# Expert weight sums on VectorE instead of GpSimd for the first two halves, and attention scores whose second term spans 128 partitions

## Chip, cores and metric

The program runs on one NeuronCore of a Trainium2 chip. The metric is the device time of one execution in microseconds. Before the change the median of three runs is 1225.96 us, from 1223.82 to 1226.51.

## What is computed

Three stages follow each other: attention with rotary position embedding, a gated feed-forward block, and a mixture of eight experts with a balanced gate.

```python
q_rot, k_rot = (rotate(q), rotate(k))          # batch 2, heads 8, 576 positions, 64 wide
scores = scale * np.matmul(q_rot, k_rot.transpose(0, 1, 3, 2))
attn = softmax(scores)                         # with +1e-9 in the denominator
x = heads_side_by_side(np.matmul(attn, v))     # 1152 x 512
a, b = x @ w1, x @ w2                          # 512 x 1024
x = ((a * b) @ w3) @ w_out                     # 1024 x 1024, 1024 x 512
P = np.exp(x @ w_gate - max)                   # 1152 x 8
for _ in range(8):
    P /= P.sum(1, keepdims=True) + 1e-09
    P /= P.sum(0, keepdims=True) + 1e-09
    P *= N / E
for e in range(8):
    out += P[:, e:e+1] * (np.maximum(x @ w1[e], 0) @ w2[e])   # 512 x 1024 x 512
```

## The kernel before

**Split numbers.** Every fp32 operand of a product is split into a high part in fp32r (a copy on ScalarE that rounds) and a low part (the difference). A product is three matmuls: high times high, high times low, low times high.

**Attention.** Two heads make a pair; there are 8 pairs, numbered 0 to 7. For each pair `load_qk` (L247) brings queries and keys with their half-swapped copies into a tile `raw` (two buffers, shared by queries and keys), `rope_mul` (L255) and `rope_add` (L259) rotate them on GpSimd, `rope_hi` (L269) makes the high part on ScalarE, and `rope_lo` the low part: for keys on GpSimd (L275), for queries on VectorE (L277). From pair 1 on, DMAs lay the parts out over 128 partitions: `spread_q` (L281) puts a head's high and low query parts one above the other in `sq`, and `spread_k` (L285) puts the head's high key part twice into `kk`, once beside each. So one matmul over 128 partitions gives high times high plus low times high. The remaining term, high query times low key, runs over the 64 partitions of the head alone: the low key part is written by `rope_lo` straight into slot 2 of `kk`, where the heads already lie on their own halves. `scores` (L312) therefore issues two matmuls of 128x128 by 288 columns and then two of 64x128 by 288 columns for each tile of 128 queries and each head; a "score step" below is these four. Pairs 1 to 7 have 5 tiles x 2 heads each, 70 score steps in all. Pair 0 takes its three terms over 64 partitions, six matmuls a step. Each step is followed by a row maximum on VectorE (L319), the exponential on ScalarE (L323), transposes on TensorE (L338), their copies out (L345) and the products with the values (L373, a 128x64 array tile).

**The order of attention** is not written by hand. The class `Plan` simulates the steps with fixed costs for each engine, ranks, and numbers of buffers (`kk` 2, `sq` 2, `raw` 2, `wide` 2 and so on) and emits the instructions in that order; each engine and the SP queue then run in that order. A step "takes" a buffer and "frees" one. The products of the two last dense weights (`w34_product`, L216 to L218) have the lowest rank and fill TensorE's gaps. Their operands come as 64-bit words and are converted by `wide_parts` on VectorE, ScalarE and GpSimd (L168 to L189).

**The experts** run as 16 steps s (expert e, half fh of the hidden width; s = 2e + fh). `prepare_first(s, u)` (L616) loads a quarter block of the first weight into `wide` (two buffers), forms four sums of 128x256 blocks into `sums` (one buffer, L625 to L628) for a seven-product scheme, and splits both into high and low parts (L125, L126). `hidden` (L681) multiplies, `project` (L729) applies the second weight and accumulates. For s = 0 `project` copies to `acc`; from s = 1 on it adds with the gate's weight (L746), so it needs the finished gate `pr`, and so does the scaling of `acc` by the first expert's weight (L835).

**The gate** is woven into step 0: `gate_start` (L778) takes one maximum over all partitions (L785) and `gate_round` (L789) runs eight times, each with one sum over all partitions, `partition_all_reduce` on GpSimd (L795), between small VectorE operations (L790 to L798). Outside attention the framework's scheduler decides the order of each engine's instructions.

Of the kernel before, what the change touches and what calls it, by code (L numbers as in the profile page):

```python
# [11 lines left out]
F32R = mybir.dt.float32r  # L12
# [94 lines left out]
def attention_two_moes(ctx: ExitStack, tc: tile.TileContext, rope, qk, v, mw12, mw3t, mwo, wg, ew1, ew2, out):  # L107
# [152 lines left out]

    def keys(n):
        if n not in K:
            K[n] = att_p.tile([P, 3, S], F32R, name="kk", bufs=2)
        return K[n]

    def rope_hi(n, w, c):
# [3 lines left out]

    def rope_lo(n, w, c, eng):
        t = raw[n, w]
        h, l = (t[:, 1, c], (t[:, 0, c].bitcast(F32R), keys(n)[:, 2])[w]) if n else (f32(QK0[w][:, 0, c]), QK0[w][:, 1, c])
        if w:
            eng.tensor_sub(l, t[:, 0, c], h)  # L275
        else:
            eng.scalar_tensor_tensor(out=l, in0=t[:, 0, c], scalar=QSCALE, in1=h, op0=ALU.mult, op1=ALU.subtract)  # L277
# [2 lines left out]

        sp.dma_start(f32(SQ[n % 2][half(x ^ j), j, :S]), raw[n, 0][half(j), 1 - x])  # L281

    def spread_k(n, j, x):

        sp.dma_start(f32(keys(n)[half(x), j]), raw[n, 1][half(j), 1])  # L285

    def half(j):
        return slice(j * D, (j + 1) * D)
# [5 lines left out]
    def scores(n, i, j):  # L294

        if j == 0:
            st["e", n, i] = att_p.tile([P, 2, S], F32, name="e", bufs=2)
            st["nm", n, i] = att_p.tile([P, 2], F32, name="nm", bufs=4)
            g, k, _ = group(i)
            if k == 0:  # L300
                st["sm", n, g] = att_p.tile([P, 3, 2], F32, name="sm", bufs=3)
        js = half(j)
        if n:
            q, k = SQ[n % 2][:, j], keys(n)
            terms = [(q, k[:, j]), (q[js], k[js, 2])]
        else:
            (qh, ql), (kh, kl) = ([t[js, x] for x in range(2)] for t in QK0)
            terms = [(qh, kh), (qh, kl), (ql, kh)]
        st["s", n, i, j] = ps = psS.tile([P, 2, 512], F32, name="s")
        for x, (q, k) in enumerate(terms):  # L310
            for h in range(2):
                pe.matmul(  # L312
                    ps[:, h, :HS], q[:, i * P : (i + 1) * P], k[:, h * HS : (h + 1) * HS],
                    start=(x == 0), stop=(x == len(terms) - 1),
                )
# [92 lines left out]
    for n in range(NP):  # L408
# [3 lines left out]
        for w in (1, 0):  # L412
            pieces = (slice(0, SF), slice(SF, S)) if n == w == 0 else (every,)
            for c in pieces:
                a, m = (n, w, c), c.stop - c.start
                r = t - 60.0 if n else -50.0 if c.start == 0 else -40.0
                r += 2 * (1 - w)
                rot = "pool" if n or c.start else "dve"
                tk = [("raw", (n, w))] if c.start == 0 else []
                step(load_qk, a, {"sp": 8 * P * m}, t - 60.0 - w if n else r - 40.0, takes=tk)  # L420
                step(rope_mul, a, {rot: 2 * m}, r, [(load_qk, *a), "tab"])
                step(rope_add, a, {rot: m}, r, [(rope_mul, *a)])
                tk = [(("sq", "kk")[w], n)] if n else []
                step(rope_hi, a, {"act": m}, r, [(rope_add, *a)], tk)
                fr = [("raw", (n, w))] if n == 0 and c is pieces[-1] else []
                step(rope_lo, a, {"pool" if n and w else "dve": m}, r, [(rope_hi, *a)], frees=fr + ([("raw", (n, 1))] if n and w else []))
            if n == 0:
                ready.append([(rope_lo, 0, w, c) for c in pieces])
                continue
            ready.append([(rope_lo, n, w, every)])  # L430
            for j, x in ((j, x) for j in range(2) for x in range(2)):
                if w:
                    step(spread_k, (n, j, x), {"sp": 4 * D * S}, t - 60.0, [(rope_hi, n, 1, every)], frees=[("raw", (n, 1))])
                else:
                    needs = [((rope_hi, rope_lo)[x], n, 0, every)]
                    step(spread_q, (n, j, x), {"sp": 4 * D * S}, t - 60.0, needs, frees=[("raw", (n, 0))])
                ready[-1].append(((spread_q, spread_k)[w], n, j, x))
        before = []
        for i in range(NQ):
            g, k, _ = group(i)  # L440
# [175 lines left out]
    def prepare_first(s, u):  # L616

        pl = wb_p if u else wa_p
        e, fh = divmod(s, 2)
        t = base.tile([P, 1024], F32, name="wide", bufs=2)  # L620
        sp.dma_start(t, ew1[e, 2 * fh + u])
        a11, a12, a22, a21 = (t[:, k * 256 : (k + 1) * 256] for k in range(4))
        sums = wa_p.tile([P, 1024], F32, name="sums")
        s1, s2, s3, s4 = (sums[:, k * 256 : (k + 1) * 256] for k in range(4))
        pool.tensor_add(s1, a21, a22)  # L625
        pool.tensor_sub(s3, a11, a21)
        pool.tensor_sub(s2, s1, a11)
        pool.tensor_sub(s4, a12, s2)  # L628
        W1[s, u] = []
        for src, n in ((t, 768), (sums, 1024)):  # L630
            h, l = (w_tile(pl, "w1") for _ in range(2))
            split_scalar_vector(h[:, :n], l[:, :n], src[:, :n])
            W1[s, u].append((h, l))
# [271 lines left out]
```

## Time and profile before

| | |
|---|---|
| median of three runs | 1225.96 us (1223.82 to 1226.51) |
| the profiled execution | 1230.79 us, of which the span of instructions is 1228.9 us |
| TensorE matmul busy | 1163.4 us, 95% of the span |
| TensorE weight loads busy | 1003.5 us, 82% |
| VectorE busy | 737.0 us, 60% |
| ScalarE busy | 427.1 us, 35% |
| GpSimd busy | 242.3 us, 20% |
| mean granted TensorE clock | 0.975 |
| score steps of pairs 1 to 7 | from 45.5 to 235.3 us |
| gate rounds | from 434.95 to 531.95 us |

Times are counted from the span's start. TensorE is busy for 95% of the whole, but that is a mean over stages: the stages with gaps, and what ends each gap, tell what a change in them is worth. A matmul's printed duration includes its way through the pipeline, so what a matmul costs TensorE is read from start to start. "PEld" is TensorE's weight load, which normally runs beside the matmul before. [...]

### The profile page before, as it was taken

What the parts mean: (1) busy time and instruction counts of PE and PEld (TensorE: products, weight loads), DVE (VectorE), ACT (ScalarE), POOL (GpSimd) and SP (SyncE); (2) the same over time, 40 slices, a digit from 0 to 9 for tenths busy, and PEclk for the clock granted to TensorE, in tenths of its full rate; (3) what the DMA queues carried; (4) which work ended last, traced back from release to release, by engine and by line L of the source; (5) the groups of instructions that cost most, each with busy time, mean ns of one, the idle gap of its engine ahead of it and who ended that gap; (6) DMA issues with size and microseconds to landing.
All of it is one profiled execution on the core that took longest, in us unless ns stands there. A gap on an engine that the chain in (4) does not pass through costs nothing.

```text
span 1228.9 us, 17324 instructions
## 1 busy us (share of the span) xinstructions
PE 1163.4 (95%) x6869; PEld 1003.5 (82%) x6869; DVE 737.0 (60%) x1324; ACT 427.1 (35%) x904; POOL 242.3 (20%) x239
## 2 busy tenths in 40 slices
PE   5889999898999999649999999999999999999998
PEld 4556666588999888638989989989889899889887
DVE  7887876587433383535665656656555655656643
ACT  3655666545332343202232232223222222322311
POOL 5646552042210001010010010010110100100100
PEclk9888999989999999869999999999999999999999
DMA  5545544054100010111111111111110111211102
GB/s 194 157 140 159 152 142 118 1 173 137 53 18 18 18 53 18 35 34 35 35 59 45 35 53 52 35 52 35 52 52 19 67 36 35 69 35 35 35 10 69
DMA packets 24993, 78.93 MB, mean 64 GB/s; under 512 B 3280, under 2 KB 3792, under 8 KB 24912
## 3 DMA queue, kind: packets, MB, share of 16 engines
q1 hardware_dynamic: 24768, 77.23, 19.9%
q8 instruction: 54, 0.88, 0.3%
q10 hardware_dynamic: 144, 0.59, 0.1%
q14 instruction: 27, 0.22, 0.1%
HBM read 67.19 MB, written 2.36 MB: 57 GB/s over the span
## 4 chain that ended last, share of the span: by engine, by line
PE 86%; DVE 6%; issue 5%; ACT 1%; POOL 1%; DMA 1%; POOLq 0%; DVEq 0%; ACTq 0%
PE z L738 11%; PE z L737 10%; PE z L739 10%; PE s L312 5%; PE T L696 4%; PE T L697 4%; PE T L698 4%; PE x L373 3%; PE t L338 3%; PE u L133 3%; PE u L131 3%; PE u L132 3%; PE Q L698 3%; PE Q L696 3%; PE Q L697 3%
## 5 line engine op out<-in xcount | busy, mean ns | idle before, releaser
L739 PE MATMUL z<-w,h 128*128 128x512 f32 x576 | 227.3, 395 | 0.0
L625 POOL TENSOR_TENSOR sums<-wide 128x256 f32<-128x256 f32 x32 | 26.8, 836 | 657.7 <-DVE w L126 335.5
L737 PE MATMUL z<-w,y 128*128 128x512 f32 x320 | 127.3, 398 | 18.6 <-DVE acc L746 18.6
L746 DVE SCALAR_TENSOR_TENSOR acc<-z,pr,acc 128x512 f32<-128x512 f32 x135 | 100.8, 748 | 56.9 <-PE z L739 56.8
L739 PEld LDWEIGHTS z<-w,h 128*128 128x128 f32 x576 | 108.6, 189 | 25.3
L738 PE MATMUL z<-w,y 128*128 128x512 f32 x320 | 127.0, 397 | 0.0
L737 PE MATMUL z<-w,h 128*128 128x512 f32 x256 | 101.5, 397 | 2.3 <-DVE acc L746 2.3
L738 PE MATMUL z<-w,h 128*128 128x512 f32 x256 | 102.0, 398 | 0.0
L125 ACT CAST w<-wide 128x768 fp32r<-128x768 f32 (+1 forms) x64 | 60.3, 943 | 94.3 <-PE z L738 62.4
L702 ACT ACTIVATE y<-tmp 128x320 fp32r<-128x320 f32 x96 | 45.0, 470 | 126.5 <-DVE tmp L718 77.4
L126 DVE TENSOR_TENSOR w<-wide,w 128x768 fp32r<-128x768 f32 (+1 forms) x64 | 69.7, 1089 | 30.0 <-ACT w L125 16.1
L702 ACT ACTIVATE h<-tmp 128x256 fp32r<-128x256 f32 x96 | 39.8, 416 | 122.1 <-DVE tmp L718 115.7
L737 PEld LDWEIGHTS z<-w,y 128*128 128x128 f32 x320 | 60.6, 189 | 25.5 <-DVE acc L746 19.0
L131 PE MATMUL u<-x,w 128*128 128x320 f32 (+1 forms) x256 | 76.8, 300 | 3.3 <-DVE gf L568 3.2
L133 PE MATMUL u<-x,w 128*128 128x320 f32 (+1 forms) x256 | 76.6, 299 | 0.0
L132 PE MATMUL u<-x,w 128*128 128x320 f32 (+1 forms) x256 | 76.1, 297 | 0.0
L338 PEld LDWEIGHTS t<-ident,e 128*128 128x128 f32 (+1 forms) x360 | 40.6, 149 | 37.0 <-issue 15.7
L319 DVE TENSOR_REDUCE nm<-s 128x1 f32<-128x576 f32 x80 | 59.6, 753 | 18.2 <-PE s L312 17.8
L312 PE MATMUL s<-kk,sq 128*128 128x288 f32 (+1 forms) x280 | 69.7, 351 | 0.2 <-ACT e L323 0.2
L338 PE MATMUL t<-ident,e 128*128 128x128 f32 (+1 forms) x360 | 59.2, 288 | 11.1 <-ACT e L323 8.2
L696 PE MATMUL T<-x,w 128*128 128x320 f32 x192 | 61.2, 319 | 5.3 <-ACT w L125 5.2
L738 PEld LDWEIGHTS z<-w,y 128*128 128x128 f32 x320 | 61.1, 191 | 6.2
(198 smaller groups left out, 3058.7 us busy)
## 6 DMA issues: line engine op xcount, KB each, us to landing
wide<-in_ew_dram SPq DMA_DIRECT2D x64, 512.0 KB, 3.5
raw<-in_qk_dram SPq DMA_DIRECT2D x15, 576.0 KB, 4.3
wide<-in_mw3t_dram SPq DMA_DIRECT2D x16, 512.0 KB, 4.6
wide<-in_mw_dram SPq DMA_DIRECT2D x16, 512.0 KB, 3.5
wide<-in_mwo_dram SPq DMA_DIRECT2D x8, 512.0 KB, 3.7
kk<-raw SPq DMA_DIRECT2D x28, 144.0 KB, 2.5
sq<-raw SPq DMA_DIRECT2D x28, 144.0 KB, 2.4
v<-in_v_dram SPq DMA_DIRECT2D x8, 320.0 KB, 4.1
```

Of the source, the lines that this page charges most:

```text
L131: pe.matmul(ps, wh, xh, start=(i == 0), stop=False)
L132: pe.matmul(ps, wh, xl, start=False, stop=False)
L133: pe.matmul(ps, wl, xh, start=False, stop=(i == n - 1))
L312: pe.matmul(ps[:, h, :HS], q[:, i * P : (i + 1) * P], k[:, h * HS : (h + 1) * HS], start=(x == 0), stop=(x == len(terms) - 1),)
L338: pe.transpose(ps[:, t, :rows], e[:rows, c : c + P], ident[:rows, :rows])
L696: pe.matmul(ps, h[:, ws], x[0], start=(first and k == 0), stop=False, **kw)
L697: pe.matmul(ps, h[:, ws], x[1], start=False, stop=False, **kw)
L698: pe.matmul(ps, l[:, ws], x[0], start=False, stop=(k == 1), **kw)
L737: pe.matmul(ps, hh[:, f, ts], wh, start=(f == 0), stop=False)
L738: pe.matmul(ps, hh[:, f, ts], wl, start=False, stop=False)
L739: pe.matmul(ps, hl[:, f, ts], wh, start=False, stop=(f == FT - 1))
L746: dve.scalar_tensor_tensor(out=acc[t], in0=ps, scalar=p, in1=acc[t], op0=ALU.mult, op1=ALU.add)
```

## The change

Two edits that touch no common code. First, for s = 0 and 1 the four block sums of `prepare_first` are issued on VectorE; from s = 2 on they stay on GpSimd. Second, the low key part is now written over the rotated key in `raw` and spread by four more DMAs per pair into two new slots of `kk`, twice like the high part. The second term of a score step becomes two matmuls over 128 partitions. It adds the product of both low parts, which before was left out. The `raw` buffer of the keys is now free when all eight spreads have landed; before it was free after four spreads and the low-part subtraction.

```diff
 def keys(n):
-            K[n] = att_p.tile([P, 3, S], F32R, name="kk", bufs=2)
+            K[n] = att_p.tile([P, 4, S], F32R, name="kk", bufs=2)
...
 def rope_lo(n, w, c, eng):
-        h, l = (t[:, 1, c], (t[:, 0, c].bitcast(F32R), keys(n)[:, 2])[w]) if n else (f32(QK0[w][:, 0, c]), QK0[w][:, 1, c])
+        h, l = (t[:, 1, c], t[:, 0, c].bitcast(F32R)) if n else (f32(QK0[w][:, 0, c]), QK0[w][:, 1, c])
...
-    def spread_k(n, j, x):
-
-        sp.dma_start(f32(keys(n)[half(x), j]), raw[n, 1][half(j), 1])
+    def spread_k(n, j, x, part):
+
+        sp.dma_start(f32(keys(n)[half(x), 2 * part + j]), raw[n, 1][half(j), 1 - part])
...
 def scores(n, i, j):
-            terms = [(q, k[:, j]), (q[js], k[js, 2])]
+            terms = [(q, k[:, j]), (q, k[:, 2 + j])]
...
                 if w:
-                    step(spread_k, (n, j, x), {"sp": 4 * D * S}, t - 60.0, [(rope_hi, n, 1, every)], frees=[("raw", (n, 1))])
+                    for part, made in enumerate((rope_hi, rope_lo)):
+                        step(spread_k, (n, j, x, part), {"sp": 4 * D * S}, t - 60.0, [(made, n, 1, every)], frees=[("raw", (n, 1))])
...
 def prepare_first(s, u):
-        pool.tensor_add(s1, a21, a22)
-        pool.tensor_sub(s3, a11, a21)
-        pool.tensor_sub(s2, s1, a11)
-        pool.tensor_sub(s4, a12, s2)
+        eng = dve if s < 2 else pool
+        eng.tensor_add(s1, a21, a22)
+        eng.tensor_sub(s3, a11, a21)
+        eng.tensor_sub(s2, s1, a11)
+        eng.tensor_sub(s4, a12, s2)
```

Lines after the edits lie two or three lower in the changed kernel: the sums are L628 to L631 there, the gate's reductions L788 and L798.

**GpSimd at the gate.** Before, the all-partition reductions (L785, L795, printed as ISA with an output) alternate with the block sums, and an ISA without an output stands at every change between the two kinds:

```order
L785 ISA
L785 ISA mg<-mx 128x1
L795 ISA cg<-cs 128x8 x2
L625 ISA
L625 TENSOR_TENSOR sums<-wide 128x256
L795 ISA
L795 ISA cg<-cs 128x8
L626 ISA
L626 TENSOR_TENSOR sums<-wide 128x256
L795 ISA
L795 ISA cg<-cs 128x8
L627 ISA
```

In the changed kernel the same place reads:

```order
L788 ISA
L788 ISA mg<-mx 128x1
L798 ISA cg<-cs 128x8 x8
L628 ISA
L628 TENSOR_TENSOR sums<-wide 128x256
```

All nine reductions now stand together; one ISA stands before them and one behind, and the first sum behind them belongs to s = 2.

**VectorE at the gate.** In the changed kernel the sums of s = 1, u = 0 stand between the splits of s = 0, u = 1 and the first sums of products (L712, in `hidden`):

```order
L126 TENSOR_TENSOR w_4243<-wide,w_4242 128x768
L126 TENSOR_TENSOR w_4247<-sums,w_4246 128x1024
L628 TENSOR_TENSOR sums<-wide 128x256
L629 TENSOR_TENSOR sums<-wide 128x256
L630 TENSOR_TENSOR sums<-sums,wide 128x256
L631 TENSOR_TENSOR sums<-wide,sums 128x256
L712 TENSOR_TENSOR tmp<-T,tmp 128x320
```

Before, L709 (the same line as L712) followed the two L126 directly; the four sums of s = 1, u = 1 are likewise strewn between later gate rounds.

**The SP queue between two pairs of attention.** Before (`kk` and `sq` are the spread keys and queries of one pair, the `raw` loads behind them bring the next):

```order
L285 DMA kk<-raw 64x576 x4
L247 DMA raw<-in_qk_dram 128x1152
L281 DMA sq_90<-raw 64x576 x3
L155 DMA wide<-in_mw3t_dram 128x1024
L281 DMA sq_90<-raw 64x576
L247 DMA raw<-in_qk_dram 128x1152
```

and in the changed kernel:

```order
L285 DMA kk<-raw 64x576 x8
L281 DMA sq_90<-raw 64x576 x4
L155 DMA wide<-in_mw3t_dram 128x1024
L247 DMA raw<-in_qk_dram 128x1152 x2
L251 DMA v_91<-in_v_dram 128x640
```

The next pair's keys were loaded behind four spreads; now both loads stand behind all twelve spreads.

## Rows read from the trace of the kernel before

**Rows 1.** Stretches: length, busy time (and count) of PE, PEld, DVE, ACT, POOL, granted clock, DMA

```profile
45.00:140.00 95.00, 87.99 (x463) 57.43 (x463) 76.72 (x108) 56.65 (x135) 54.20 (x35) 0.87 0.52 157
140.00:235.00 95.00, 94.85 (x570) 63.19 (x570) 65.25 (x116) 59.69 (x145) 34.38 (x25) 1.00 0.37 106
300.00:420.00 120.00, 120.00 (x901) 120.00 (x900) 48.09 (x100) 38.54 (x92) 11.42 (x12) 1.00 0.10 31
430.00:460.00 30.00, 29.86 (x198) 27.08 (x197) 25.11 (x74) 13.31 (x27) 3.03 (x5) 1.00 0.17 54
487.00:556.00 69.00, 42.52 (x212) 36.36 (x211) 31.08 (x77) 11.32 (x21) 8.33 (x13) 0.80 0.12 39
```

**Rows 2.** What TensorE waited for between 420 and 560 us: total, times, longest

```profile
PE z L737 <- DVE acc L746: 20.9, 2, 18.6
PE T L696 <- ACT w L125: 5.2, 1, 5.2
```

**Rows 3.** GpSimd's timeline at the gate: start, duration, operation, idle before it

```profile
478.84 0.73 POOL L627 TENSOR_TENSOR sums<-sums,wide 128x256 f32<-128x256 f32 x1 [7.32 <-issue]
485.80 1.29 POOL L795 PARTITION_ALL_REDUCE cg<-cs  x1 [6.23 <-issue]
495.12 0.71 POOL L628 TENSOR_TENSOR sums<-wide,sums 128x256 f32<-128x256 f32 x1 [8.04 <-issue]
...
531.52 0.43 POOL L795 PARTITION_ALL_REDUCE cg<-cs  x1 [6.23 <-issue]
```

**Rows 4.** First and last of the three busy stretches at half clock, columns as in rows 1

```profile
496.90:502.30 5.40, 5.34 (x19) 4.93 (x20) 1.77 (x3) 0.01 (x1) 0.00 (x0) 0.50 0.24 93
...
550.30:553.60 3.30, 3.30 (x12) 2.93 (x11) 0.58 (x2) 0.00 (x0) 0.00 (x0) 0.50 0.02 5
```

**Rows 5.** The chain that ended last, 45 to 238 us, by line

```profile
by line: PE s L312 25.2%; PE x L373 19.8%; PE t L338 18.4%; issue 6.4%; PE w L216 6.1%; PE w L218 4.2%; PE w L217 4.2%; DVE cvu L176 3.5%; PE t L360 3.2%; DVE cvu L173 1.7%; DVE raw L277 1.6%; DVE sm L351 1.5%; DVE rb L354 1.5%; DVE nm L319
```

**Rows 6.** TensorE's timeline, one score step of pair 3 and what follows

```profile
101.92 0.96 PE L312 MATMUL s<-kk,sq 128*128 128x288 f32 x4
...
102.36 0.29 PEld L312 LDWEIGHTS s<-kk,sq 64*128 64x128 f32 x2 [0.16 <-issue]
...
102.81 0.19 PEld L216 LDWEIGHTS w<-y 128*128 128x128 f32 x1 [0.16 <-issue]
102.82 0.50 PE L216 MATMUL w<-y 128*128 128x512 f32 x1
```

**Rows 7.** The same timeline, a score step of pair 0: six matmuls over 64 partitions

```profile
38.63 1.06 PE L312 MATMUL s<-x 64*128 64x288 f32 x6
39.62 0.50 PE L216 MATMUL w<-y 128*128 128x512 f32 x1
```

**Rows 8.** Line L312: duration min/median/max in ns, first and last start

```profile
L312 PE MATMUL s<-kk,sq x280: 284/376/608, 45.5 to 235.3; 128*128 128x288 f32 x70, 64*128 64x288 f32 x70
```

**Rows 9.** Groups of instructions that prepare queries and keys: total, mean ns, idle before

```profile
L255 POOL TENSOR_TENSOR raw<-raw,tab 128x1152 f32<-128x1152 f32 (+1 forms) x15 | 40.6, 2706 | 13.0 <-DMA raw<-in_qk_dram 13.0
L259 POOL TENSOR_TENSOR raw<-raw 128x576 f32<-128x576 f32 (+1 forms) x15 | 23.2, 1544 | 1.0
L275 POOL TENSOR_TENSOR kk<-raw 128x576 fp32r<-128x576 f32 x7 | 10.1, 1443 | 14.1 <-ACT raw L269 14.1
L277 DVE SCALAR_TENSOR_TENSOR raw<-raw 128x576 fp32r<-128x576 f32 x7 | 9.6, 1374 | 0.0
```

**Rows 10.** Their DMAs: issue min/median/max in ns; KB and us to landing

```profile
L285 SPq DMA_DIRECT2D kk<-raw x28: 461/594/982, 24.4 to 188.9; - x28
...
raw<-in_qk_dram SPq DMA_DIRECT2D x15, 576.0 KB, 4.3
kk<-raw SPq DMA_DIRECT2D x28, 144.0 KB, 2.5
```

**Rows 11.** The block sums on GpSimd (total, mean ns), and like operations on VectorE (start, duration)

```profile
L625 POOL TENSOR_TENSOR sums<-wide 128x256 f32<-128x256 f32 x32 | 26.8, 836 | 657.7 <-DVE w L126 335.5
...
418.67 0.42 DVE L603 TENSOR_TENSOR f<-z,f 128x256 f32<-128x256 f32 x1 [1.23 <-PE z L133]
419.01 0.41 DVE L604 TENSOR_TENSOR f<-z,f 128x256 f32<-128x256 f32 x1
```

More of the change, by code (lines that the diff above doesn't have):

```diff
@@ L425, in attention_two_moes @@
                 fr = [("raw", (n, w))] if n == 0 and c is pieces[-1] else []
-                step(rope_lo, a, {"pool" if n and w else "dve": m}, r, [(rope_hi, *a)], frees=fr + ([("raw", (n, 1))] if n and w else []))
+                step(rope_lo, a, {"pool" if n and w else "dve": m}, r, [(rope_hi, *a)], frees=fr)
             if n == 0:
@@ L432, in attention_two_moes @@
                 if w:
-                    step(spread_k, (n, j, x), {"sp": 4 * D * S}, t - 60.0, [(rope_hi, n, 1, every)], frees=[("raw", (n, 1))])
+                    for part, made in enumerate((rope_hi, rope_lo)):
+                        step(spread_k, (n, j, x, part), {"sp": 4 * D * S}, t - 60.0, [(made, n, 1, every)], frees=[("raw", (n, 1))])
+                        ready[-1].append((spread_k, n, j, x, part))
                 else:
@@ L436, in attention_two_moes @@
                     step(spread_q, (n, j, x), {"sp": 4 * D * S}, t - 60.0, needs, frees=[("raw", (n, 0))])
-                ready[-1].append(((spread_q, spread_k)[w], n, j, x))
+                    ready[-1].append((spread_q, n, j, x))
         before = []
```

## The prediction

> **What bounds the kernel now.** I read the stretches first, then what TensorE waits for, then GpSimd's timeline, and for attention the chain that ended last. TensorE is the bound almost everywhere: between 300 and 420 us it runs 901 matmuls in 120 us without a gap [rows 1]. Two stretches matter for this change.
>
> The gate. From 487 to 556 us TensorE is busy for 42.52 of 69 us, at a mean clock of 0.80 [rows 1]. Two waits hold most of the gap: 20.9 us until VectorE's accumulation L746, and 5.2 us until the weight split L125 [rows 2]. Behind both stands GpSimd. Its last block sum for s = 1 starts at 495.12 us, and L125 needs it; its last reduction starts at 531.52 us, and the gate's weights, which L746 needs, come after it [rows 3]. Neither is long (0.4 to 1.3 us), but each has 6.2 to 8.0 us of idle time in front that no other engine explains ("issue"), at every place where a sum follows a reduction or a reduction a sum [rows 3]. In the printed order an ISA instruction without an output stands exactly there. So GpSimd pays some 7 us for each change of kind, and before the change it alternates behind the third reduction.
>
> Attention. Between 140 and 235 us TensorE is busy for 94.85 of 95 us at full clock; between 45 and 140 us for 87.99 of 95, at a clock of 0.87 [rows 1]. The score steps L312 are the largest line of the chain, 25.2% of the 193 us from 45 to 238 [rows 5].
>
> **The change part by part.**
>
> *Reductions together.* The changed order has two changes of kind instead of one at nearly every reduction. The first lies between the last weight conversion and the gate, long before the maximum is ready; the second behind the last reduction, before the sums of s = 2. What remains of a round is its VectorE work and one reduction, so the gate should be done soon after step 0's hidden products. Both waits then go: 20.9 + 5.2 = 26.1 us. The clock follows. [...] Together 31.6 us.
>
> *Sums on VectorE.* 16 operations of 128x256. GpSimd's take 0.836 us; VectorE starts two like ones 0.34 us apart [rows 11], so 16 x 0.34 = 5.4 us of VectorE. Eight of them (s = 0) run during the feed-forward stage, where VectorE is busy for 48.09 of 120 us [rows 1]; I cost them at nothing, and if VectorE were full there they would cost 2.7 us. The other eight fall into 426 to 460 us, where VectorE is busy for 25.11 of 30 us while TensorE is full [rows 1]. Behind them in VectorE's order wait L712 and L706, whose outputs free TensorE's PSUM tiles. Between nothing and their whole 2.7 us I take 1.6. The gate part gives 31.6 - 1.6 = **30 us**. What is late next is TensorE itself: the sums of s = 2 stay on GpSimd, behind one change of some 7 us, but are needed only after all of step 1.
>
> *Score steps over 128 partitions.* A step takes 0.90 us from start to start (101.92 to 102.82) [rows 6]. Four matmuls of 288 columns at 0.133 us are 0.53 us. The rest, 0.37 us, stands at two places: the weight load of the 64-partition term starts 0.16 us late, and so does the first 128-partition load behind it [rows 6]. A step of pair 0, six matmuls all over 64 partitions, takes 0.99 us with one such passage behind it [rows 7]: 6 x 0.133 = 0.80, and 0.19 for one passage. The two readings agree on 0.19 us for a passage between array shapes. In the changed order 55 of the 70 steps meet only 128x128 neighbours behind them and lose both passages; 15 are followed by value products or half-high transposes and lose one. That is 55 x 0.37 + 15 x 0.19 = 23 us of TensorE's time.
>
> How much of it reaches the end? 25.2% of 193 us is 48.6 us of chain [rows 5], or 54 steps of 0.90; at the mean saving of 0.33 us that is 17.8 us, if no other chain comes up. One does: VectorE is busy for 76.72 of 95 us in the first half [rows 1]. I take three quarters, **13 us**. The bounds are 0 (all given back to the queues) and 23.
>
> [...] In rows 1, 900 weight loads and 901 matmuls, all 128x128, fill the same 120 us, so a load hides beside the running matmul. [...]
>
> *More spreads.* 28 more DMAs, 28 x 0.594 = 16.6 us more issue time on the SP queue [rows 10] over 190 us. Behind the eight key spreads of a pair stand its query spreads, the next weight load and both `raw` loads of the next pair; SP must now also wait for the low part (1.44 us on GpSimd). The loop that this closes: load 4.3 us [rows 10]; on GpSimd both rotations and the low keys, 2 x 2.71 + 2 x 1.54 + 1.44 = 9.9; the low queries on VectorE 1.4 [rows 9]; four query spreads 2.4; landing 2.5 [rows 10]. That is 20.5 us, or 25.3 if the eight key spreads (4.8) aren't hidden, plus waits in the engines' queues. A pair now takes 189.8 / 7 = 27.1 us [rows 8], and at my 13 us it would take 25.2. So the loop fits, barely; this is why I don't take more than 13.
>
> **Sum.** 30 + 13 = 43 us from the profiled execution's 1230.79 gives 1187.8. That execution is 4.8 us above the median of the runs, so against 1225.96 I forecast **1183 us**.
>
> **The rivals.**
> - *The whole of TensorE's saving arrives* (chance 0.15). For it: 94.85 of 95 us busy in the second half. Against it: VectorE in the first. 30 + 23 us: 1173.
> - *The loop through `raw` takes over* (0.19). It decides when queue waits exceed 25.2 - 20.5 = 4.7 us a pair. For it: both loads now stand behind all twelve spreads. Against it: 94.85 of 95 us busy in the second half, so keys came in time there. Attention gains 0 to 5 us: about 1193.
> - *VectorE holds step 0* (0.05). 25.11 of 30 us is close to full; were its in-order waits for each reduction to stop L712 and L706 too, a round could cost 1 us of TensorE: 8 us of the 30 gone, 1191.
> - *The changes of kind stay* (0.02): the reductions are slow by themselves. Against it: two in a row stand together in the old order, and the waits are found only beside sums. Only attention gains: 1213.
> - *Slower* (0.02): the same loop starves TensorE. To pay back 30 us a pair must exceed 27.1 + 30 / 7 = 31.4 us, that is 6 us of queue waits on top of the wholly serial 25.3; at 33 us a pair the time is 1226 - 30 + 41 = 1237. [...]
> - *Weight loads do not hide* (0.02): a load of 0.19 us [rows 6] on top of each matmul makes a step 4 x 0.32 = 1.29 us, 0.39 more than now, 27 us for 70 steps; with the gate's 30 about 1223. [...]
>
> **How the numbers follow.** The forecast keeps 0.55. Its own range is 1176 to 1191 (gate 26 to 32, attention 9 to 18). The range given reaches to 1171 (gate 32, attention 23) and to 1200 (gate 26, attention nothing), which leaves out the last three rivals and a part of the tails. A measurement of this kernel tells about 0.2% (2.5 us) from no change. Slower by more: 0.02, the rival that starves TensorE. Within: 0.01, half of the last rival, whose 1223 lies just at that bound. Faster by more: 0.97.
>
> **What would show it.** Right: nine reductions of the changed kernel without 6 to 8 us between them; TensorE without a gap over 2 us from the end of step 0 through step 1, at clock 1.00; score steps 0.53 us apart where transposes follow; attention's last score step near 222 us instead of 235. Wrong: score steps still 0.9 us apart; a new wait of TensorE on `kk` or `sq`, or a lower clock between 100 and 235 us; TensorE waiting for L712 or L706 between 410 and 450 us.

## The result, and the profile after

| | before | after |
|---|---|---|
| median of four runs each, in one set | 1226.24 us (1223.82 to 1230.56) | 1191.99 us (1190.13 to 1195.27) |
| ratio to before, 95% interval | | 0.972, 0.9685 to 0.9755 |
| the profiled execution, its span | 1230.79, 1228.9 us | 1191.73, 1189.9 us |
| TensorE matmul busy | 1163.4 us, 95% | 1137.2 us, 96% |
| VectorE busy | 737.0 us, 60% | 749.2 us, 63% |
| GpSimd busy | 242.3 us, 20% | 230.7 us, 19% |
| mean granted clock | 0.975 | 0.989 |

The change gains 34 us where 43 were forecast: 1192 us lies in the range that was given, above the forecast's own 1176 to 1191. (Two kernels are best compared by their ratios, since each set of runs has its own runs of the kernel before, with medians from 1226.2 to 1227.4 us. One execution of e10, below, took 1580.77 us at a granted clock of 0.658 and is left out of its median.)

Three places divide the profiled span. The last low part of attention (L396) ends at 244.3 us before and 238.8 after; the first reduction of the gate starts at 434.95 and 428.22; the spans end at 1228.9 and 1189.9. So attention gave 5.5 us, the feed-forward stage 1.3, and everything from the gate on 32.3. (These are the profiled executions. Before's lies 4.6 us above its median and after's at it, so the three add up to 39 and not to 34.)

**The gate.** GpSimd's timeline after the change (start, duration, operation, idle before it):

```profile
431.49 0.59 POOL L798 PARTITION_ALL_REDUCE cg<-cs  x1 [2.90 <-DVE cs L797]
...
461.62 0.40 POOL L798 PARTITION_ALL_REDUCE cg<-cs  x1 [2.11 <-DVE cs L797]
488.27 1.04 POOL L628 TENSOR_TENSOR sums<-wide 128x256 f32<-128x256 f32 x1 [26.26 <-ACT y L705]
```

The nine reductions now follow each other 2.5 to 5.3 us apart, and the eight of L798 wait for VectorE's column sums and for nothing else. The 6 to 8 us of "issue" in [rows 3] are gone. The last reduction starts at 461.62 instead of 531.52 us. What TensorE still waits for between 225 and 570 us, the kernel after (total, times, longest; waits of 0.3 us and less left out but for the one on L712):

```profile
PE u L216 <- ACT y L186: 5.4, 1, 5.4
PE u L131 <- DVE gf L570: 3.2, 3, 2.3
PE z L778 <- DVE y L126: 1.5, 1, 1.5
PE T L699 <- DVE tmp L712: 0.3, 1, 0.3
```

Both waits of [rows 2] have left the list; its largest three lie ahead of the first reduction. The stretches of the kernel after, columns as in [rows 1]:

```profile
45.00:140.00 95.00, 79.22 (x489) 55.01 (x489) 80.66 (x116) 56.17 (x133) 57.28 (x35) 0.93 0.58 174
140.00:235.00 95.00, 87.69 (x564) 63.79 (x566) 73.64 (x119) 60.33 (x145) 37.50 (x27) 0.98 0.46 130
430.00:460.00 30.00, 29.51 (x181) 26.28 (x180) 27.34 (x95) 14.37 (x27) 3.29 (x7) 1.00 0.21 68
420.00:560.00 140.00, 139.23 (x831) 124.73 (x829) 92.67 (x227) 47.67 (x92) 16.09 (x25) 1.00 0.16 50
40.00:238.80 198.80, 173.16 (x1089) 122.49 (x1088) 159.65 (x244) 120.02 (x286) 96.26 (x62) 0.96 0.51 149
```

and of the kernel before, for the last two (attention from 40 us to its end, and the gate):

```profile
40.00:244.30 204.30, 191.85 (x1086) 125.67 (x1084) 150.18 (x234) 121.73 (x293) 93.28 (x62) 0.94 0.42 124
420.00:560.00 140.00, 111.92 (x632) 97.39 (x631) 69.77 (x181) 38.35 (x76) 17.31 (x25) 0.90 0.11 34
```

From 420 to 560 us TensorE is now busy for 139.23 of 140 us at full clock, against 111.92 at 0.90.

**Attention.** TensorE's timeline after the change:

```profile
219.20 0.78 PE L312 MATMUL s<-kk,sq 128*128 128x288 f32 x4
219.81 0.39 PE L216 MATMUL w<-y 128*128 128x512 f32 x1
...
221.77 1.31 PE L312 MATMUL s<-kk,sq 128*128 128x288 f32 x8
222.93 0.38 PE L360 MATMUL t<-ident,rb 128*128 128x128 f32 x2
```

A step takes 0.61 us from start to start, or 1.16 for two, where it took 0.90 [rows 6]. Over all steps of pairs 1 to 7 the median is 0.62 us, before 0.90. The saving is there, and TensorE is busy for 18.7 us less in attention (191.85 to 173.16). But its idle time there grew from 12.5 to 25.6 us, so 13 of the 18.7 went into waits. Between 140 and 235 us it finished 564 matmuls where it finished 570 before [rows 1], in 87.69 busy us instead of 94.85: faster steps, no more work done. The waits of its matmuls between 45 and 210 us that come to 1 us or more, first before, then after:

```profile
PE t L338 <- ACT e L323: 5.8, 4, 3.4
PE t L360 <- DVE rb L354: 1.5, 2, 1.1
```

```profile
PE t L338 <- ACT e L323: 10.1, 11, 2.6
PE t L360 <- DVE rb L354: 9.1, 4, 4.8
PE t L338 <- DVE et L345: 2.9, 3, 1.0
```

No wait on `kk` or `sq` is among them, or among the shorter ones. Two are VectorE's own outputs, `rb` and `et`. The exponentials `e` come from ScalarE, and ScalarE waits for VectorE in turn: for the row maximum (11.4 us between 45 and 235 us before, 14.7 after), and with its rounding copy L186, which stands in one queue with the exponentials, for the last VectorE operation of a conversion, L181. That wait trebled (before, then after):

```profile
ACT y L186 <- DVE cvu L181: 5.8, 5, 1.8
```

```profile
ACT y L186 <- DVE cvu L181: 17.3, 11, 3.7
```

The chain that ended last, 45 to 235 us, says the same of the kernel after:

```profile
by line: PE x L373 14.3%; PE t L338 11.4%; issue 10.8%; PE s L312 9.9%; DVE nm L319 8.0%; DVE cvu L176 6.5%; DVE cvu L181 4.9%; DVE et L345 4.5%; ACT e L323 4.4%; PE w L216 4.2%; DVE cvu L173 3.5%; PE w L217 3.2%; PE w L218 3.2%; DVE rb L35
```

The score step fell from 25.2% [rows 5] to 9.9%. VectorE's row maximum, its three conversion operations (L173, L176, L181) and its eviction L345 (the copy of transposed blocks out of PSUM) now hold 27.4%. VectorE itself became busier, 159.65 us in a shorter stage instead of 150.18. Its groups up to 255 us (total, mean ns), before and after:

```profile
L345 DVE COPY et<-t 128x384 f32<-128x384 f32 (+1 forms) x45 | 24.3, 541 | 24.5 <-PE t L338 24.1
L176 DVE SCALAR_TENSOR_TENSOR cvu<-wide,cvu 128x512 int32<-128x512 int32 x24 | 23.9, 1002 | 0.6
L181 DVE SCALAR_TENSOR_TENSOR cvu<-cvy,cvu 128x512 int32<-128x512 int32 x24 | 21.3, 886 | 2.7 <-ACT cvy L168 1.4
```

```profile
L176 DVE SCALAR_TENSOR_TENSOR cvu<-wide,cvu 128x512 int32<-128x512 int32 x26 | 30.1, 1159 | 0.7
L181 DVE SCALAR_TENSOR_TENSOR cvu<-cvy,cvu 128x512 int32<-128x512 int32 x25 | 28.7, 1149 | 3.1 <-ACT cvy L168 1.8
L345 DVE COPY et<-t 128x384 f32<-128x384 f32 (+1 forms) x54 | 28.6, 536 | 17.4 <-PE t L338 17.3
```

Two things moved. The planner counts a score step at the same TensorE time in both kernels (4 x 288 columns), but it has four more spreads a pair to place and a `raw` buffer that is free later; it ordered the rest anew and gave VectorE nine more evictions, 54 instead of 45. And the conversion operations grew longer, though nothing in them changed. Why they do so stands in the two timelines side by side, VectorE's and then GpSimd's, both of the kernel after:

```profile
159.48 1.79 DVE L176 SCALAR_TENSOR_TENSOR cvu<-wide,cvu 128x512 int32<-128x512 int32 x1
161.37 2.95 DVE L181 SCALAR_TENSOR_TENSOR cvu<-cvy,cvu 128x512 int32<-128x512 int32 x1
...
167.09 1.42 DVE L351 TENSOR_SCALAR sm<-sm 128x4 f32<-128x4 f32 x1 [0.57 <-ACT e L323]
```

```profile
159.24 1.48 POOL L259 TENSOR_TENSOR raw<-raw 128x576 f32<-128x576 f32 x1
160.67 3.11 POOL L255 TENSOR_TENSOR raw<-raw,tab 128x1152 f32<-128x1152 f32 x1
...
167.06 1.42 POOL L259 TENSOR_TENSOR raw<-raw 128x576 f32<-128x576 f32 x1
```

L351 works on four numbers per partition, and takes 1.42 us: as long as the GpSimd operation that started 0.03 us ahead of it. L176 and L181 start while GpSimd is in L259 and L255, and end 0.5 to 0.6 us behind their ends. This holds for all fourteen operations of L176 and L181 between 40 and 240 us that take over 0.8 us: each starts within a GpSimd operation and ends 0.54 or 0.55 us behind that operation's end. Where VectorE starts first nothing is lost: L176 at 108.24 us, 0.17 us ahead of an L255, takes 0.69 us. Of a line the minimum is what the operation costs alone, the maximum what it costs behind a GpSimd operation (kernel after, up to 240 us: min/median/max in ns; L345, L351 and L354 have two sizes):

```profile
L176 DVE SCALAR_TENSOR_TENSOR cvu<-wide,cvu x21: 674/693/3036, 15.9 to 239.5; 128x512 int32<-128x512 int32 x21
L319 DVE TENSOR_REDUCE nm<-s x80: 739/747/759, 13.7 to 230.4; 128x1 f32<-128x576 f32 x80
L345 DVE COPY et<-t x54: 356/548/558, 21.3 to 230.0; 128x384 f32<-128x384 f32 x50, 128x192 f32<-128x192 f32 x4
L351 DVE TENSOR_SCALAR sm<-sm x16: 155/170/1421, 24.1 to 232.5; 128x4 f32<-128x4 f32 x8, 128x6 f32<-128x6 f32 x8
L354 DVE COPY rb<-sm x16: 293/454/2444, 24.5 to 232.9; 128x256 f32<-128x256 f32 x8, 128x384 f32<-128x384 f32 x8
```

L319 and L345 read PSUM, and never vary beyond their shape, although between 40 and 240 us at least 23 of L319 and 14 of L345 start while a GpSimd operation runs. L176, L351 and L354 read SBUF, and reach four to nine times their shortest. So one of these three that starts behind a GpSimd operation lasts until that one has ended: L176 takes 3.04 us behind an L255 of 2.85 us, where it takes 0.69 alone. What in the chip makes it wait, and why L319 and L345 don't, no row says.

So two accounts of the lost attention gain were on the table. **VectorE theory**: VectorE, with its operations held up beside GpSimd, sets the pace of a pair. **Loop theory**, the prediction's second rival: the chain load, rotate, split, spread through the two `raw` buffers sets it. The trace also speaks for the loop: the last query spread of pair 5, for one, is issued at 151.8 us and lands some 2.3 us later, and the pair's first step starts at 156.18, so by timing alone either could be late.

### The profile page after: what moved, and what is told of

It is laid out like the page before. It is cut to its first block, busy times and chain, and to the rows that moved or that the text cites. A ratio compares the mean times of both kernels' runs of the same rounds, so it can differ in the third digit from the quotient of the medians.

```text
span 1189.9 us, 17349 instructions
## 1 busy us (share of the span) xinstructions
PE 1137.2 (96%) x6869; PEld 995.1 (84%) x6869; DVE 749.2 (63%) x1349; ACT 424.9 (36%) x895; POOL 230.7 (19%) x223
## 4 chain that ended last, share of the span: by engine, by line
PE 85%; DVE 10%; issue 3%; ACT 1%; DMA 1%; POOL 1%; DVEq 0%; ACTq 0%; POOLq 0%
PE z L741 11%; PE z L740 11%; PE z L742 11%; PE T L699 4%; PE T L700 4%; PE T L701 4%; PE u L131 3%; PE u L132 3%; PE u L133 3%; PE Q L701 3%; PE Q L699 3%; PE Q L700 3%; PE A L701 3%; PE A L700 3%; PE A L699 3%; PE x L373 3%
## 5 line engine op out<-in xcount | busy, mean ns | idle before, releaser
L628 POOL TENSOR_TENSOR sums<-wide 128x256 f32<-128x256 f32 x28 | 23.5, 839 | 574.8 <-DMA wide<-in_ew_dram 281.7
L742 PEld LDWEIGHTS z<-w,h 128*128 128x128 f32 x576 | 107.9, 187 | 25.2
L126 DVE TENSOR_TENSOR w<-wide,w 128x768 fp32r<-128x768 f32 (+1 forms) x64 | 69.6, 1088 | 26.5 <-PE T L701 14.8
L319 DVE TENSOR_REDUCE nm<-s 128x1 f32<-128x576 f32 x80 | 59.2, 750 | 13.4 <-PE s L312 13.3
L323 ACT ACTIVATE e<-s,nm 128x576 f32<-128x576 f32 x80 | 59.3, 743 | 18.6 <-DVE nm L319 17.3
L706 DVE SCALAR_TENSOR_TENSOR h<-tmp,y 128x320 fp32r<-128x320 f32 x96 | 46.9, 489 | 26.0 <-ACT y L705 25.8
```

The lines of the kernel that those rows point to most:

```text
L742: pe.matmul(ps, hl[:, f, ts], wh, start=False, stop=(f == FT - 1))
```

## The experiments

Twelve kernels, in three sets of four. "Attention ends" is the end of the last L396 (the same line under another number where an edit moves it) in the one execution that was profiled. It scatters by some us: the same attention ended at 244.3 and 242.1 us (before, e1) and at 238.8, 237.0 and 241.3 us (after, e2, e12).

| run | median, us | ratio to before | attention ends, us |
|---|---|---|---|
| before | 1226.2 | | 244.3 |
| after | 1192.0 | 0.9720 (0.9685 to 0.9755) | 238.8 |
| e1_gate_only | 1195.2 | 0.9741 (0.9728 to 0.9755) | 242.1 |
| e2_scores_only | 1221.2 | 0.9953 (0.9939 to 0.9966) | 237.0 |
| e3_raw3 | 1195.7 | 0.9741 (0.9723 to 0.9758) | 242.1 |
| e4_nosign | 1175.6 | 0.9575 (0.9562 to 0.9589) | 223.4 |
| e5_before_nosign | 1217.0 | 0.9915 (0.9890 to 0.9941) | 231.3 |
| e6_norope | 1169.4 | 0.9523 (0.9497 to 0.9548) | 212.8 |
| e7_costs | 1187.2 | 0.9672 (0.9646 to 0.9698) | 235.0 |
| e8_nolow | 1171.4 | 0.9538 (0.9512 to 0.9563) | 223.6 |
| e9_best | 1172.0 | 0.9542 (0.9515 to 0.9569) | 221.9 |
| e10_best_raw3 | 1176.9 | 0.9583 (0.9558 to 0.9607) | 229.9 |
| e11_more_pool | 1201.8 | 0.9785 (0.9761 to 0.9809) | 249.0 |
| e12_gate_switch | 1193.1 | 0.9699 (0.9663 to 0.9735) | 241.3 |

**e1, the gate's part alone.** The kernel before with

```diff
-        pool.tensor_add(s1, a21, a22)
+        eng = dve if s < 2 else pool
+        eng.tensor_add(s1, a21, a22)
```

and the other three sums likewise.

> The kernel before with only the weight sums of the first two halves on VectorE; attention as before. If the two parts of the change add up and the gate part is worth the 30 us of the prediction, this runs at about 1196 us (0.975 of before), with the last score step at 235 us as before and no wait for the counts between 430 and 560 us. Rival, that part of the 34 us of the whole change came from the scores after all (the 13 us of the prediction) and the gate gave only 21: 1205 us.

Measured: 1195.2 against 1227.1 us in the same set, 31.9 us (30 to 33 by the interval). The rival's 1205 is out.

**e2, the scores' part alone.** The kernel after with

```diff
-        eng = dve if s < 2 else pool
+        eng = pool
```

> The changed kernel with the weight sums back on GpSimd; only the attention scores are changed. By the trace of the change the attention ended some 5 us earlier: about 1221 us (0.996). If the scores gave 13 us as predicted and the gate less: 1213 us (0.989). The waits at the gate, some 26 us in all, should be there as in the kernel before.

Measured: 5.9 us (4.2 to 7.5). The waits at the gate are back (TensorE between 420 and 560 us):

```profile
PE z L740 <- DVE acc L749: 19.0, 2, 18.5
PE T L699 <- ACT w L125: 2.7, 1, 2.7
```

The parts add up to 38 us, the whole change measured 30 to 39. The gate came as forecast and the scores' part is the one that was mis-sized.

**e3, relief for the loop.**

```diff
-            raw[n, w] = att_p.tile([P, 2, S], F32, name="raw", bufs=2)
+            raw[n, w] = att_p.tile([P, 2, S], F32, name="raw", bufs=3)
-        st["r", n, g] = r = att_p.tile([P, 3, P], F32, name="r", bufs=2)
+        st["r", n, g] = r = att_p.tile([P, 3, P], F32, name="r", bufs=1)
```

with the planner's counts to match.

> The changed kernel with three buffers for the raw queries and keys instead of two (room for it is made by one buffer less for the small tile r), and the planner told of both. Loop theory (the chain load, rotation, split, spread through the two raw buffers sets the pace of a pair): the spreads of the queries land well before their pair starts and the attention ends 6 to 15 us earlier than the changed kernel's 238.8 us, so 1177 to 1186 us. VectorE theory (its 81 to 87% busy time, with operations stretched where GpSimd runs beside it, sets the pace): the spreads come earlier but the end of the attention moves by less than 2 us.

Measured: 1195.7 us, no gain. Line L312 of this kernel and of the kernel after (duration in ns, first and last start):

```profile
L312 PE MATMUL s<-kk,sq x280: 290/297/607, 47.7 to 233.8; 128*128 128x288 f32 x140
```

```profile
L312 PE MATMUL s<-kk,sq x280: 290/297/607, 43.6 to 230.0; 128*128 128x288 f32 x140
```

Pairs 1 to 7 take 186.1 us with three buffers and 186.4 with two; before the change they took 189.8 [rows 8]. Differences of a few us say nothing here: the same attention as in the kernel after took 191.3 us for these pairs in e12. But the 6 to 15 us of the loop theory are out. The run is not clean, though: the planner ordered the rest anew, pair 1 starts 4.1 us later, and VectorE makes 43 evictions instead of 54 and is busy for 5 us less, which brought nothing either. The clean test of both theories is e4.

**e4, relief for VectorE.** In the planner's loop over the conversions, the second VectorE operation does nothing:

```diff
-            plan.step((load, u, k), {e: m}, rank, lambda e, k=k: got[u][2][k](), needs, tk, fr)
+            plan.step((load, u, k), {e: m}, rank, (lambda e: None) if k == 2 else lambda e, k=k: got[u][2][k](), needs, tk, fr)
```

> The changed kernel without the sign operation in the conversions that lie beside the attention (L176 there: VectorE's conversion takes one operation less for each of 20 blocks; the converted weights lose their signs, and nothing else is left out; order of everything else as it was). That takes some 20 operations of 0.7 to 3.0 us, mean 1.35, so up to 27 us of VectorE's 152 us between 45 and 230 us. VectorE theory: the attention ends 6 to 12 us earlier. Loop theory: by 0 to 2 us.

Measured: 1175.6 us, 16 us below the kernel after (18 by the ratios), and the attention ends 15.5 us earlier. That is more than the 6 to 12 expected, and the loop theory's 0 to 2 is out. Nothing else moved in any engine's order, so one operation per conversion is worth 16 us: VectorE sets the pace. A part of it reaches TensorE through ScalarE, whose copy L186 waits for L181 for 9.4 us here (45 to 220 us) and for 17.3 in the kernel after; the run doesn't tell the two ways apart.

**e5, the same on the kernel before.**

> The kernel before without the sign operation in the conversions beside the attention (the converted weights lose their signs, nothing else is left out). The changed kernel gained 16 us from leaving it out. If VectorE became the bound of the attention only through the cheaper score step, the kernel before gains clearly less, 0 to 5 us: 1222 to 1227 us, and the scores' change is worth 16 to 20 us once VectorE has room. If VectorE held the attention of the kernel before as much, it gains 12 us or more, 1215 us or less, and the scores' change stays at some 6 us with or without the sign.

Measured: 9 us below the kernel before (7 to 13 by the interval), between the two cases. VectorE held a part of the attention before the change too. Without the sign operation the scores' change is worth 0.9915 - 0.9575 - 0.0259 (the gate, e1) = 0.0081, 10 us, instead of 6. With the three intervals added as squares that is 6 to 14 us, which still meets e2's 4.2 to 7.5, so a larger worth is likely but not shown. The 16 to 20 expected of a VectorE with room did not come; that it still lacks room fits this, and is not shown by it.

**e6, GpSimd out of the way.**

```diff
-                step(rope_mul, a, {rot: 2 * m}, r, [(load_qk, *a), "tab"])
-                step(rope_add, a, {rot: m}, r, [(rope_mul, *a)])
+                if n == 0:
+                    step(rope_mul, a, {rot: 2 * m}, r, [(load_qk, *a), "tab"])
+                    step(rope_add, a, {rot: m}, r, [(rope_mul, *a)])
+                else:
+                    plan.step((rope_mul, *a), {rot: 2 * m}, r, lambda e: None, [(load_qk, *a), "tab"])
+                    plan.step((rope_add, *a), {rot: m}, r, lambda e: None, [(rope_mul, *a)])
```

> The changed kernel without the two GpSimd operations that rotate queries and keys of pairs 1 to 7 (the rotation is left out there; all else is computed, on unrotated values). That takes some 28 of GpSimd's operations away beside the attention. If VectorE's conversion operations are stretched by GpSimd running beside them (L181 0.6 to 0.7 us alone, 1.25 us in the mean), L176 and L181 fall to 0.7 to 0.9 us in the mean, VectorE's busy time between 45 and 230 us falls by 12 to 18 us, and the attention ends 5 to 12 us earlier: 1180 to 1187 us. If their length has nothing to do with GpSimd, they stay at 1.2 to 1.4 us and the time at 1190 to 1193 us.

Measured: 1169.4 us, 23 us below the kernel after, twice what was expected. The same groups of VectorE as above, 45 to 225 us of this kernel:

```profile
L176 DVE SCALAR_TENSOR_TENSOR cvu<-wide,cvu 128x512 int32<-128x512 int32 x20 | 15.7, 790 | 0.5
L181 DVE SCALAR_TENSOR_TENSOR cvu<-cvy,cvu 128x512 int32<-128x512 int32 x19 | 14.8, 781 | 3.2 <-ACT cvy L168 2.3
```

VectorE's own operations, untouched, fell to 0.79 and 0.78 us, from 1.35 and 1.25 between 45 and 230 us of the kernel after. So their length does come from GpSimd. How much of the 23 us that is can't be told from this run alone, because the rotation is also a part of the loop; e3 and e10 gave no sign that the loop is worth anything there.

**e7, the planner's costs corrected.**

```diff
-            ("dve", WU // 2, (), ["cvu"], []),
-            ("dve", WU, (1,), [], ["wide"]),
-            ("dve", WU, (0, 2), [], ["cvy"]),
+            ("dve", 620, (), ["cvu"], []),
+            ("dve", 1230, (1,), [], ["wide"]),
+            ("dve", 1130, (0, 2), [], ["cvy"]),
```

> The changed kernel with the planner's VectorE sizes of the three conversion operations set to what the trace of it measured (0.72, 1.35 and 1.25 us instead of 0.34, 0.60 and 0.60), so that the planner hands more evictions of transposed blocks to ScalarE. VectorE theory: VectorE's share falls, ScalarE's rises from 62%, the attention ends 2 to 8 us earlier, 1184 to 1190 us. Rival, that the planner's order matters more than the balance, or ScalarE becomes late: within 2 us of the changed kernel's 1192 us or above it.

Measured: 1187.2 us, 5 us below the kernel after, inside the expected 2 to 8 (the intervals of the two ratios still overlap a little). VectorE's evictions up to 255 us:

```profile
L345 DVE COPY et<-t 128x384 f32<-128x384 f32 (+1 forms) x29 | 15.6, 541 | 14.9 <-PE t L338 14.5
```

29 instead of 54; the rest went to ScalarE (91 instead of 66). VectorE is busy for 12 us less in attention (147.76 against 159.65 from 40 us to its end), and only 5 us came of it: the sum of VectorE's time is not what counts, but which of its outputs is late.

**e8, one VectorE operation less in every conversion.** Sign masked in one single-input operation, low bits dropped:

```diff
-            dve.tensor_scalar(u, low, 29, None, op0=ALU.logical_shift_right)
+            dve.tensor_scalar(u, high, -(2**31), None, op0=ALU.bitwise_and)
 
         def signed():
-            dve.scalar_tensor_tensor(
-                out=u, in0=high, scalar=-(2**31), in1=u, op0=ALU.bitwise_and, op1=ALU.bitwise_or
-            )
+            pass
```

> The changed kernel with two VectorE operations per conversion instead of three in all conversions: the lowest three of the 23 fraction bits of each converted weight are left out, so the operation that shifts them (L173) and the one that joins the sign to them (L176) become one that masks the sign, with a single input. Beside the attention VectorE loses 20 operations of 1.35 us. VectorE theory: about what leaving out the sign gave, 1174 to 1180 us. Loop theory: 1190 to 1192 us.

Measured: 1171.4 us, 55 us below the kernel before and 21 below the kernel after. The attention ends where it did in e4, at 223.6 us; the 4 us beyond e4 come behind it, where e8 saves the operation as well. Of the twelve this is the fastest that still computes the whole, at the price of three fraction bits of the converted weights.

**e9 and e10, what is next.** e8 with the measured costs (the lines against the kernel after, beside e8's own edit), in e10 with three `raw` buffers too:

```diff
-            ("dve", WU // 2, (), ["cvu"], []),
-            ("dve", WU, (1,), [], ["wide"]),
-            ("dve", WU, (0, 2), [], ["cvy"]),
+            ("dve", 650, (), ["cvu"], ["wide"]),
+            ("dve", 1100, (0, 1), [], ["cvy"]),
```

> Both reliefs of VectorE together: two operations per conversion (the lowest three fraction bits of the converted weights are left out) and the planner's sizes for them as measured (0.75 and 1.22 us). Alone they gave 20.6 and 4.8 us. If VectorE still holds the attention with the first relief, they add up in part: 1166 to 1170 us. If something else holds it by then (ScalarE, or the loop through the raw buffers), within 2 us of 1171 us.

> The kernel of the run before this one with three raw buffers (and one buffer less for r). With VectorE as the bound three raw buffers did nothing (1195.7 against 1192.0 us). If the loop through the raw buffers is what holds the attention once VectorE has room, it is now worth 3 us or more against the run before; if VectorE or ScalarE still hold it, it is again within 3 us of that run or slower.

Measured: 1172.0 us, no better than e8, and 1176.9 with three buffers, 4.9 us worse. The two reliefs don't add up, and the loop isn't what is next either. What is next stays open.

**e11, more GpSimd work on no chain.** `spare` is a tile that nobody reads; `more` holds for the conversions beside the attention.

```diff
             pool.tensor_sub(l, f32(u), f32(h))
+            if more:
+                pool.tensor_sub(spare[:, :WU], tab[:, 0, :WU], tab[:, 1, :WU])
```

> The changed kernel with one more GpSimd operation (a subtraction of two table rows into a tile that nobody reads, 128x512, some 1.3 us) behind each of the 20 conversions beside the attention: 26 us more GpSimd, on no chain of data, where GpSimd is half idle. Stretching theory: VectorE's operations beside it grow by 0.3 to 0.5 us per us of GpSimd, so VectorE is 8 to 13 us busier and the attention ends 4 to 10 us later: 1196 to 1202 us. If GpSimd's work only matters through the rotation's own chain: 1190 to 1194 us, VectorE's L176 and L181 as before at 1.35 and 1.25 us.

Measured: 1201.8 us, 10 us above the kernel after (8 by the ratios); the attention ends 10 us later. TensorE never waited for GpSimd; its waits that grew are for VectorE's `rb` (11.1 us, in the kernel after 9.1) and `et` (8.2, 2.9, both from 45 to 235 us). But the growth isn't where it was expected: the conversions did not grow (1.20 and 1.14 us in the mean between 45 and 230 us, in the kernel after 1.35 and 1.25), while VectorE's normalisation grew (L355 and L358 here, L351 and L354 in the kernel after):

```profile
L358 DVE COPY rb<-sm 128x256 f32<-128x256 f32 (+1 forms) x16 | 17.2, 1073 | 0.5
L355 DVE TENSOR_SCALAR sm<-sm 128x4 f32<-128x4 f32 (+1 forms) x16 | 12.8, 801 | 2.5 <-ACT e L327 2.5
```

In the kernel after the same 16 took 0.777 and 0.493 us in the mean: 9.7 us more together.

**e12, does every GpSimd operation between reductions cost a change of kind?**

```diff
-        pool.partition_all_reduce(cg, cs, P, bass_isa.ReduceOp.add)
+        pool.tensor_copy(cp, cs)
+        pool.partition_all_reduce(cg, cp, P, bass_isa.ReduceOp.add)
```

> The changed kernel with a GpSimd copy of the eight column sums (128x8) ahead of each of the eight reductions of the normalisation, so that kinds alternate again. By the prediction's reading each change of kind costs 6 to 8 us: every reduction and every copy is preceded by 6 to 8 us in which GpSimd waits for nothing the profile shows, a round takes some 15 us instead of 4, the last reduction comes near 545 us instead of 462, and TensorE waits 50 to 85 us more: 1240 to 1275 us. If the cost falls only on the way into a reduction: last reduction near 500 us and 1200 to 1225 us. If the kinds don't matter and the cost was the sums' own: 1192 to 1196 us.

Measured: 1193.1 us, no cost. GpSimd's timeline there:

```profile
453.14 0.19 POOL L799 COPY cp<-cs 128x8 f32<-128x8 f32 x1 [4.66 <-DVE cs L798]
453.43 0.40 POOL L800 PARTITION_ALL_REDUCE cg<-cp  x1
457.42 0.25 POOL L799 COPY cp<-cs 128x8 f32<-128x8 f32 x1 [3.60 <-DVE cs L798]
```

A reduction starts 0.09 to 0.10 us behind its copy, and the next copy 2.5 to 4.9 us behind the reduction, with only VectorE's work in between. So a copy is not a change of kind; the block sums, two-input operations, were. The ISA instruction without an output, which stands at each change in the kernel before, is in the trace a pair of MODIFY_POOL_CONFIG, an instruction of GpSimd's sequencer, which busy times leave out. At the reductions of the kernel before:

```profile
L795 POOLq MODIFY_POOL_CONFIG  x12: 1/3/11, 450.8 to 525.5; - x12
```

These are six pairs, one for each of the six reductions of L795 that follow a sum, and seven more pairs stand at the sums that follow a reduction; 5.6 to 8.1 us pass from a pair to the next operation. In the kernel after there is one pair long ahead of the first reduction (at 317.0 us), one behind the last (462.0), and none in between. The 0.10 us ahead of a reduction and the 2.5 to 4.9 us ahead of a copy in e12 leave no room for 5.6 us either. So the time stands behind a pair of this instruction, and a copy of 128x8 does not bring it. That the sums themselves are slow, the third case, doesn't fit [rows 3], where the 6.23 us stand ahead of reductions too. A small two-input operation in the copy's place was not tried.

## Why the prediction was right and where it was wrong

- **The gate, 30 us: right.** (One reading was too neat: the idle times at a change begin at 5.84 us and not at 6.2, and the profile puts three of the six ahead of L795 down to VectorE and not to "issue".) Both waits are gone, the clock is 1.00, and the part alone measured 32 us. The sum's 31.6 us hold 5.5 us for the clock beyond the 26.1 of the waits; no run shows this term by itself. Measured were a clock of 0.50 in the stretches of [rows 4], in the first of which matmuls of 320 columns start 0.27 us apart against 0.15 at clock 1.00 (kernel before, at 499 and at 700 us), and from 420 to 560 us a mean clock of 0.90 before and 1.00 after. The 1.6 us set aside for VectorE's extra sums were not seen: between 430 and 460 us VectorE is busy for 27.34 of 30 us, yet TensorE waits only 0.3 us for L712. The rivals "VectorE holds step 0" and "the changes of kind stay" fell.
- **TensorE's saving, 23 us: nearly right.** It was 18.7. The step was put at 0.53 us by the mean matmul of another stage, 0.133 us for 288 columns (901 matmuls in 120 us [rows 1]); in the rows above it takes 0.58 to 0.61, or 0.145 to 0.15 per matmul. The two passages between array shapes were worth some 0.3 us of a step together, not 0.37.
- **The weight loads hide: right.** With each load of 0.19 us on top of its matmul a step would have taken 1.29 us, by the prediction's estimate from [rows 6]; it takes 0.61 in the row above, with its four 128x128 loads in it.
- **"I take three quarters, 13 us": the step that failed.** 5.5 to 6 us arrived, under a third of 18.7; the last score step starts at 230.0 us instead of near 222. The share of the chain, 25.2%, was read as if the next chain lay well below. It lay just below: between 140 and 235 us, where TensorE was 99.8% busy, the same number of matmuls got done in less busy time and no less time. VectorE's busy share was in the rows and was one of the two reasons given for not taking all (the other was the loop through `raw`); but it was read as a number of its own, when L176 already took 1.00 us in the mean where 0.69 is what it takes alone, with GpSimd's rotation beside it, and when the planner would hand VectorE nine more evictions. One of the prediction's own signs of being wrong came, if faintly: the clock between 100 and 235 us fell from 1.00 to 0.99 (0.97 in e2 and 0.96 in e12, with the same attention).
- **The rival with the right time had the wrong cause.** "The loop through `raw` takes over" forecast 0 to 5 us of attention and about 1193 us; 5.5 to 6 and 1192 came. Three `raw` buffers did nothing (e3) or worse (e10); an operation less on VectorE gave 16 us (e4) and 20 more operations on a half idle GpSimd cost 8 to 10 (e11). A result that meets a rival's number is no proof of its mechanism.
- **The slower rival** needed that loop to starve TensorE; in the kernel after no wait of TensorE on a `kk` or `sq` spread is longer than 0.3 us, and in the twelve runs none is longer than 0.7 (e8).

Open: how e6's 23 us divide between shorter VectorE operations and a shorter rotation, what holds the attention below 222 us, what the new scores would give in the old order (nine evictions less are 4.9 us of VectorE; this was not run), and what the new score step would give with VectorE quite free.

## What to carry to other kernels

That an engine is busy for 99% of a stage (here 94.85 of 95 us) says nothing of how far the next limit lies: before a saving there is counted in full, take the next engine's work away in a test, or price how its operations lengthen beside others. Compare the mean of an operation with its median in the same group: a mean well above the median, with a maximum of four times as much (L176: 1.16, 0.69 and 3.04 us), was time lost to another engine here, and the busy share hid it. On GpSimd, look for MODIFY_POOL_CONFIG between operations (here 5.6 to 8.1 us passed from a pair of them to the next operation), and keep operations of a kind together, above all around a chain that other engines wait for.

## What the hardware showed that was not expected

- VectorE's operation on 128x4 numbers takes 0.16 us alone and 1.42 us beside a GpSimd operation of 1.42 us that started 0.03 us earlier. The 128x512 operations go from 0.69 to 3.0 us. L319 and L345, which read PSUM, keep their time to within 20 ns for a shape beside the same GpSimd work (739 to 759 ns, and 541 to 558 at 128x384).
- GpSimd's 6 to 8 us between reductions and two-input sums, behind a pair of MODIFY_POOL_CONFIG each time, do not arise between reductions and a copy of 128x8: the reduction starts 0.10 us behind the copy.
- Twenty more GpSimd operations of 1.37 us in the mean, on no chain of data, cost the kernel 8 to 10 us.
